# Side loads pinned in the queue, and a first pass of 18 groups in place of 19

## The chip, the cores and the metric

The kernel runs on one core of one Trainium2 chip. The metric is the device time of an execution in microseconds (us). The core's engines are TensorE (PE), VectorE (DVE), ScalarE (ACT), GpSimd (POOL) and SyncE (SP); here SP issues every transfer, so that SP's queue is the one order in which loads and stores start.

## The reference

Banded attention over q, k, v makes x (3072 x 512). A layer of 8 experts with dense routing follows; `P` is a softmax of `x @ w_gate` that is balanced by 8 rounds of row and column scaling.

```python
x = np.ascontiguousarray(attn_out.transpose(0, 2, 1, 3)).reshape(B * S, H * D)
...
    for e in range(E):
        h = np.maximum(x @ w1[e], 0.0)
        ye = h @ w2[e]
        out += P[:, e:e + 1] * ye
```

w1 is 8 x 512 x 1024, w2 is 8 x 1024 x 512, all of it float32.

## The kernel before

Every float32 operand is split into a high and a low part, and a product is three matmuls (high x low, low x high, high x high). Rows are handled in three blocks of 1024. The hidden dimension is cut into groups of 256; one group (two hidden tiles of one expert) was done during the attention already, so that 31 groups are left, numbered 0 to 30 (expert 0 has 3, each other expert 4).

Within a group both layers can use Strassen's scheme of seven products. Layer 1 always does: 7 products of 6 matmuls of 128x512, in the order x, y, x, z, w, z, w by the name of the PSUM bank. For layer 2 there are two forms. The **first pass** (block 2, `for g in range(SPLIT)`) uses the plain form: 8 row tiles of 6 matmuls (`y_ps`). The **later passes**, listed in `order`, are block 0 and block 1 with groups 0 to 30 each, and then the **return** of block 2 with groups `SPLIT` to 30; they use seven products of 6 matmuls in layer 2 (`m_ps`). TensorE alternates: a product of layer 1 of group g, then a piece of layer 2 of group g-1.

The later passes take the weights already summed, split and stored to DRAM (`w1s[g]`, `w2s[g]`). Who makes them:

- For groups below `SPLIT`, `make(g)` in the first pass, one group ahead: loads `w1f` and `w2f` (lines 740, 741), casts on ACT (L745), sums (L763) and low parts (L746) on POOL, and stores from `w1ops`, `w2ops`, `s2ops` (lines 790, 795, 796). It is needed by the first pass itself.
- For groups from `SPLIT` on, **side halves**: one half is the w1 or the w2 part of a group. `side_half` loads 512 KB into `raw` (L1454 for w2, L1461 for w1), a piece of `acc`. `quick` treats them beside the first pass: high parts (L1475, ACT), four sums on POOL (L763, `acc<-acc`), low parts (L1479, DVE), the high part of the sums (L1506, ACT, written over `raw`), their low part (L1508, DVE), and three stores: own parts (L1486, from `own`), high sums and low sums (both L1490, from `acc`). There is one `raw`, so that the next load waits until the store of the high sums has landed. `SPLIT - FIRST_SIDE - 1` halves are quick; the rest is `slow`, beside the pass of block 0, one half every two groups.

In the text the first load of `quick` stands in group 3 at step 6, each half is worked on in the group after its load, and its stores are at steps 4 and 5.

A scheduler orders each engine's instructions by its own estimate of when inputs are ready. `tc.keep_in_program_order(ins)` takes that freedom from one instruction in one direction: it is queued behind the instruction that stands just ahead of it in the text on the same engine. The matmuls are so pinned, and so are the first loads of the pass of block 0: `moe.in_order = True` holds when `load_first(w1s[0], ...)` and `load_x` are called, after the first pass. These are seven loads `w1r<-w1s` of 256 KB and seven loads `xr<-xs` of 1 MB (both L805).

`weights_of(n)` loads one expert's routing weights for a block (L1604, `acc<-p_dram`, 512 KB) into one of two pieces of `acc`; the piece for the first turn is the one that was `raw`.

Of the kernel before, what the change touches and what calls it, by code (L numbers as in the profile page):

```python
# [17 lines left out]
P = 128  # L18
# [21 lines left out]
FG = 2  # L40
# [1 line left out]
LATE = 2  # L42
TURNED = (0, 0, 1, 3, 4, 6, 7, 7)
FREE = 5
SPLIT = 19
FIRST_SIDE = 3
LOAD = 25
SIDE_END = 20
# [69 lines left out]
class Banded:  # L118
# [449 lines left out]
    def keep(self):  # L568

        if self.ended is None:  # L570
            return
        o_ps, g, x = self.ended
        self.ended = None
        of = o_ps.rearrange("p t c -> p (t c)")
        for xh, xl, src, dst, width, _ in x:
            self.nc.scalar.copy(out=xh[:, g, dst:dst + width], in_=of[:, src:src + width])
        for _, _, src, _, _, whole in x:
            if whole is not None:
                n, dst = whole[0], whole[1](g)
                self.nc.scalar.copy(out=dst, in_=of[:, src:src + n * P].rearrange("p (t q) -> p t q", q=P))  # L580
        for xh, xl, src, dst, width, _ in x:
            self.nc.vector.tensor_tensor(out=xl[:, g, dst:dst + width], in0=of[:, src:src + width],
                                         in1=xh[:, g, dst:dst + width], op=ALU.subtract)
# [11 lines left out]
class Dense:  # L595
# [19 lines left out]
    keep = flush  # L615
# [470 lines left out]
def pipeline(tc, attention, ident, moe, acc):  # L1086


    nc = tc.nc
    KT, KH, DM, NU, E = moe.KT, moe.KH, moe.DM, moe.NU, moe.E  # L1090
# [4 lines left out]
    groups = [(0, f) for f in range(NF0, FT, FG)] + [(e, f) for e in range(1, E) for f in range(0, FT, FG)]  # L1095
    NG = len(groups)
    PLAIN = NG - 1
    with ExitStack() as top:
# [227 lines left out]
        def make(g):  # L1326
            if g < SPLIT and g not in wts:
                s = staged if g == 0 else moe.stage_group(*groups[g], stage)
                wts[g] = moe.make_group(s, wpools[g % 2], spool[0], stage, w1s[g], w2s[g])
# [42 lines left out]
        def plain_ops():  # L1372
            hs = {}

            def ended(name, bank):
                hs[name] = hop.tile([P, 2, BU], F32R, name="hop")
                moe.relu_split(bank, hs[name])
            return hs, ended
# [66 lines left out]

        scratch = []

        def side_half(g, second):

            e, f = groups[g]  # L1450
            raw, sums, pair = (t.rearrange("p t d -> p (t d)") if n < 2 else t for n, t in enumerate(scratch[-1]))
            if second:
                src = moe.w2[e, f * P:(f + FG) * P, :].rearrange("(f p) d -> p f d", p=P)
                nc.sync.dma_start(out=raw.rearrange("p (f d) -> p f d", d=DM), in_=src)  # L1454
                rows = raw.rearrange("p (f e d) -> p f e d", f=2, e=2)
                a11, a12, a21, a22 = rows[:, 0, 0], rows[:, 1, 0], rows[:, 0, 1], rows[:, 1, 1]
                own = [((pair[:, 0, i], pair[:, 1:3, i]), (a11, rows[:, 1])) for i in range(2)]
                s = sums.rearrange("p (n d) -> p n d", n=4)
            else:
                src = moe.w1[e, :, f * P:(f + FG) * P].rearrange("(c p) f -> p c f", p=P)  # L1460
                nc.sync.dma_start(out=raw.rearrange("p (c f) -> p c f", f=FG * P), in_=src)  # L1461
                rows = raw.rearrange("p (o c e f) -> p o c e f", o=2, c=KH, e=FG)
                a11, a12, a21, a22 = rows[:, 0, :, 0], rows[:, 1, :, 0], rows[:, 0, :, 1], rows[:, 1, :, 1]
                wide = pair.rearrange("p o s (c f) -> p o s c f", f=P)
                own = [((wide[:, 0:2, i], wide[:, 2, i]), (rows[:, :, :, 0], a22)) for i in range(2)]
                s = sums.rearrange("p (n c f) -> p n c f", n=4, f=P)
            plain, more = second and g >= PLAIN, None
            if plain:
                more = sums[:, 0:2 * HD].bitcast(F32R).rearrange("p (s d) -> p s d", s=2)
                own = [((*t, more[:, i]), (*x, a21)) for i, (t, x) in enumerate(own)]  # L1470
            return raw, sums, pair, s, own, (a11, a12, a21, a22), plain, more

        def own_his(own):
            for t, x in zip(*own[0]):
                nc.scalar.copy(out=t, in_=x)  # L1475

        def own_lows(own, engine, keep=lambda ins: ins):
            for hi, lo, x in zip(own[0][0], own[1][0], own[1][1]):
                keep(engine.tensor_tensor(out=lo, in0=x, in1=hi, op=ALU.subtract))  # L1479

        def store_own(g, second, pair, more):
            if more is not None:
                nc.sync.dma_start(out=w2p[g - PLAIN][:, 0:3].bitcast(F32), in_=pair.bitcast(F32))
                nc.sync.dma_start(out=w2p[g - PLAIN][:, 3].bitcast(F32), in_=more.bitcast(F32))
            else:
                nc.sync.dma_start(out=(w2s if second else w1s)[g][:, 4:7].bitcast(F32), in_=pair.bitcast(F32))  # L1486

        def store_sums(g, second, part, t):
            dst = (w2s if second else w1s)[g][:, 0:4, part]
            nc.sync.dma_start(out=dst.bitcast(F32), in_=t.rearrange("p (n d) -> p n d", n=4))  # L1490

        def quick(halves):

            for g, second in halves:
                while (yield) != 6:
                    pass
                raw, sums, pair, s, own, parts, plain, more = side_half(g, second)
                while (yield) != 0:
                    pass
                own_his(own)  # L1500
                moe.left_sums(s, *parts, 0, 2)
                yield
                own_lows(own, nc.vector)
                moe.left_sums(s, *parts, 2, 4)
                yield
                nc.scalar.copy(out=raw.bitcast(F32R), in_=sums)  # L1506
                yield
                nc.vector.tensor_tensor(out=sums.bitcast(F32R), in0=sums, in1=raw, op=ALU.subtract)  # L1508
                while (yield) != 4:
                    pass  # L1510
                store_sums(g, second, 0, raw)
                store_own(g, second, pair, more)
                yield
                store_sums(g, second, 1, sums)
            scratch.append(None)
            while True:
                yield
# [37 lines left out]
        def beside(steps):  # L1555
            next(steps)
            return steps.send

        halves_late = [(g, second) for g in range(SPLIT, NG) for second in range(2)]
        quick_ones = SPLIT - FIRST_SIDE - 1  # L1560

# [6 lines left out]
        next(sinkhorn)  # L1568
        next(prev)
        side = beside(quick(halves_late[:quick_ones]))  # L1570
        for g in range(SPLIT):
            hs, ended = plain_ops() if g else lead
# [5 lines left out]
            def each(n):  # L1578
# [3 lines left out]
                if g > FIRST_SIDE or (g == FIRST_SIDE and n == 6):  # L1582
                    side(n)
                    if g > 3 and kept:
# [4 lines left out]
            prev = second_plain(b, g, w2, hs, lambda k: yps.tile([P, DM], F32, name="y_ps", tag="y"),  # L1589
                                g == SPLIT - 1, False, store=part_tile)  # L1590
        for _ in sinkhorn:
            pass
        for _ in turned:
            pass
        order = [(n, 0) for n in range(NB - 1)] + [(NB - 1, SPLIT)]
        cells = [(q, g) for q, (_, first) in enumerate(order) for g in range(first, NG)]
# [3 lines left out]
        def weights_of(n):  # L1600
            if n < len(turns) and turns[n] not in pbc:
                q, e = turns[n]
                t = acc[:, BT + 2 * (n % 2):BT + 2 * (n % 2) + 2]
                nc.sync.dma_start(out=t, in_=p_dram[order[q][0], :, e].rearrange("i j p -> i (j p)").partition_broadcast(P))  # L1604
                pbc[q, e] = t
# [34 lines left out]
        for q, (b, first) in enumerate(order):  # L1640
            x_ops, x_next = x_next, {}
            ms = {}
            for g in range(first, NG):
                e = groups[g][0]
                if g > first and groups[g - 1][0] == e:
                    weights_of(turns.index((q, e)) + 1)
                w = first_w.pop(g)
                if g < PLAIN:
# [89 lines left out]
def kernel(  # L1738
# [33 lines left out]
    with tc.If(rv > 0) as cmp:  # L1772
        pipeline(tc, band, ident, moe, acc)
    with cmp.Else():
        pipeline(tc, Dense(tc, q, k, v, ng, nl), ident, moe, acc)
# [32 lines left out]
```

## Time and profile before

| | |
|---|---|
| median of 3 runs | 2089.2 us (2088.31 to 2090.33) |
| the profiled execution, its own time | 2087.19 us |
| its span, from the first to the last instruction | 2085.2 us |
| PE busy | 2069.4 us, 99% of the span |
| POOL, DVE, ACT busy | 1609.1, 1541.7, 764.3 us |
| mean transfer rate | 248 GB/s |

The span is the profile's time axis; 2.0 us of the execution's own time lie outside it. The attention ends near 250 us, the first pass runs from there to 644.37 us, where the first matmul of block 0's pass starts. In a line of the timeline the numbers are start and duration in us, then engine, line, operation, tile written and tiles read; `[t <-X]` is idle time of the engine just before, and what ended it.

### The profile page before, as it was taken

The numbers are of one execution on the slowest core, as the hardware profiler recorded it, in microseconds if no ns is written. First come the engines' busy times: TensorE is split into PE (matmuls) and PEld (weight loads), VectorE is DVE, ScalarE is ACT, GpSimd is POOL, SyncE is SP. The second block draws the span as 40 slices with busy tenths as digits, with TensorE's granted clock in tenths as the row PEclk, the third lists the DMA queues.
The fourth block names the chain that finished last, engine by engine and source line by source line (L and its number), as shares of the span: only waits on it lengthen the run. The fifth ranks groups of instructions, "written<-read, shape, count | busy, mean of one in ns | idle before, by whom it ended". The sixth has DMA issues, their size and how long they took to land.

```text
span 2085.2 us, 31822 instructions
## 1 busy us (share of the span) xinstructions
PE 2069.4 (99%) x10401; PEld 1714.4 (82%) x10402; DVE 1541.7 (74%) x2291; ACT 764.3 (37%) x1604; POOL 1609.1 (77%) x1430
## 2 busy tenths in 40 slices
PE   9999999999999999999999999999999999999998
PEld 6888877888888888888888888888888888888887
DVE  7777688777775777777777775777777777767777
ACT  7898735444432322322322224222222222232221
POOL 5687698999973898998777776777777777767776
PEclk9999999999999999999999999999999999999999
DMA  6897798999989888888877788777777777797772
GB/s 145 203 234 213 235 376 310 346 340 353 335 317 368 282 251 265 266 255 276 267 204 194 204 304 282 202 203 200 199 203 204 194 204 204 219 365 204 193 194 91
DMA packets 351517, 516.15 MB, mean 248 GB/s; under 512 B 117297, under 2 KB 187121, under 8 KB 342385
## 3 DMA queue, kind: packets, MB, share of 16 engines
q1 hardware_dynamic: 351344, 514.02, 78.8%
q8 instruction: 87, 1.43, 0.3%
q14 instruction: 86, 0.70, 0.1%
HBM read 365.19 MB, written 148.73 MB: 246 GB/s over the span
## 4 chain that ended last, share of the span: by engine, by line
PE 96%; DVE 2%; POOL 1%; ACT 1%; DMA 0%; issue 0%; SPq 0%; ACTq 0%; POOLq 0%; DVEq 0%
PE m_ps L112 32%; PE y_ps L112 12%; PE bank_z L112 12%; PE bank_w L112 12%; PE bank_x L112 12%; PE bank_y L112 6%; PE o_ps L112 2%; PE s_ps L112 2%; PE t_ps L115 2%; PE h_ps L112 1%; PE tp L115 1%; PE r_ps L115 1%; PE c_ps L115 1%; DMA w1f<-in_moe_w_dram 0%; PE g_ps L112 0%
## 5 line engine op out<-in xcount | busy, mean ns | idle before, releaser
L112 PE MATMUL m_ps<-hop,w2r 128*128 128x512 f32 x2982 | 756.7, 389 | 0.0
L1709 DVE TENSOR_TENSOR m<-m_ps,m 128x1024 f32<-128x1024 f32 x476 | 580.4, 1220 | 228.8 <-PE m_ps L112 224.4
L112 PEld LDWEIGHTS m_ps<-hop,w2r 128*128 128x128 f32 x2982 | 559.8, 188 | 116.3
L1039 POOL TENSOR_TENSOR hop<-h,hop 128x512 fp32r<-128x512 f32 x213 | 276.8, 1299 | 294.8 <-ACT hop L1045 294.8
L1039 POOL TENSOR_TENSOR hop<-hsum,hop 128x512 fp32r<-128x512 f32 x284 | 362.0, 1298 | 2.9 <-ACT hop L1045 2.5
L1045 ACT CAST hop<-hsum 128x512 fp32r<-128x512 f32 x284 | 175.9, 622 | 467.7 <-POOL hsum L1039 464.3
L1045 ACT CAST hop<-h 128x512 fp32r<-128x512 f32 x213 | 132.4, 621 | 442.1 <-DVE h L1061 429.7
L112 PE MATMUL y_ps<-w2ops,hop 128*128 128x512 f32 x912 | 230.2, 391 | 2.3 <-DVE hop L882 2.3
L112 PE MATMUL bank_w<-xr,w1r 128*128 128x512 f32 x888 | 225.8, 390 | 0.0
L112 PE MATMUL bank_z<-xr,w1r 128*128 128x512 f32 x888 | 225.7, 389 | 0.0
L112 PE MATMUL bank_x<-xr,w1r 128*128 128x512 f32 x888 | 225.5, 389 | 0.0
L1039 POOL TENSOR_TENSOR hsum<-h,h 128x512 f32<-128x512 f32 x142 | 181.2, 1298 | 44.9 <-DVE h L1061 44.8
L112 PEld LDWEIGHTS y_ps<-w2ops,hop 128*128 128x128 f32 x912 | 171.7, 188 | 38.7 <-DVE hop L882 2.6
L112 PEld LDWEIGHTS bank_x<-xr,w1r 128*128 128x128 f32 x888 | 166.5, 188 | 34.5
L112 PEld LDWEIGHTS bank_w<-xr,w1r 128*128 128x128 f32 x888 | 166.4, 188 | 34.4
L112 PEld LDWEIGHTS bank_z<-xr,w1r 128*128 128x128 f32 x888 | 166.4, 188 | 34.4
L1039 POOL TENSOR_TENSOR hsum<-h,hsum 128x512 f32<-128x512 f32 x142 | 184.6, 1300 | 0.0
L1398 DVE SCALAR_TENSOR_TENSOR acc<-y_ps,pm,acc 128x512 f32<-128x512 f32 x152 | 113.2, 746 | 59.7 <-PE y_ps L112 59.1
L112 PE MATMUL bank_y<-xr,w1r 128*128 128x512 f32 x444 | 112.7, 389 | 0.0
L408 ACT ACTIVATE p_sb<-p_sb,mx 128x256 f32<-128x256 f32 (+1 forms) x192 | 93.6, 497 | 17.9 <-DVE mx L390 17.1
L112 PEld LDWEIGHTS bank_y<-xr,w1r 128*128 128x128 f32 x444 | 83.3, 188 | 17.3
L917 DVE TENSOR_TENSOR t<-bank_y,t 128x512 f32<-128x512 f32 x93 | 64.2, 690 | 38.2 <-PE bank_y L112 37.8
(224 smaller groups left out, 2977.9 us busy)
## 6 DMA issues: line engine op xcount, KB each, us to landing
w1r<-w1s SPq DMA_DIRECT2D x518, 256.0 KB, 3.0
w2r<-w2s SPq DMA_DIRECT2D x497, 256.0 KB, 3.0
w1s<-w1ops SPq DMA_DIRECT2D x19, 1792.0 KB, 7.2
w2s<-s2ops SPq DMA_DIRECT2D x19, 1024.0 KB, 7.7
w2s<-w2ops SPq DMA_DIRECT2D x19, 768.0 KB, 8.1
acc<-in_moe_w_dram SPq DMA_DIRECT2D x24, 512.0 KB, 5.7
w1s<-acc SPq DMA_DIRECT2D x24, 512.0 KB, 6.3
xr<-xs_t SPq DMA_DIRECT2D x12, 1024.0 KB, 11.2
```

Of the source, the lines that this page charges most:

```text
L112: return self.tc.keep_in_program_order(self.engine.matmul(*args, **kw))
L115: return self.tc.keep_in_program_order(self.engine.transpose(*args, **kw))
L408: nc.scalar.activation(out=pv, in_=pv, func=AF.Exp, bias=mx[:, u:u + 1], scale=-1.0, accum_out=sm[:, i, j:j + 1])
L917: tt(out=t, in0=bank["y"], in1=t, op=ALU.add)
L1039: ins = self.nc.gpsimd.tensor_tensor(out=out, in0=x, in1=y, op=ALU.subtract)
L1045: self.rounded = self.nc.scalar.copy(out=t[:, 0], in_=self.full[name])
L1398: nc.vector.scalar_tensor_tensor(out=a, in0=y_ps, scalar=moe.pm[:, tt, e:e + 1], in1=a, op0=ALU.mult, op1=ALU.add)
L1709: evicted[:] = [nc.vector.tensor_tensor(out=ms[p], in0=bank, in1=ms[p], op=ALU.add)]
```

## The change

`SPLIT` goes from 19 to 18: the first pass does 18 groups, the return 13 in place of 12, and side halves are made for groups 18 to 30: 26 in place of 24, of which 14 (before: 15) are quick and 12 (before: 9) are slow. The loads of `quick` go through `keep_in_program_order`; those of `slow` don't. The condition of `weights_of` is widened so that a pass that begins with the last group of an expert (group 18 is that of expert 4) also fetches the next expert's weights.

```diff
-SPLIT = 19
+SPLIT = 18
...
-        def side_half(g, second):
+        def side_half(g, second, keep=lambda ins: ins):
...
-                nc.sync.dma_start(out=raw.rearrange("p (f d) -> p f d", d=DM), in_=src)
+                keep(nc.sync.dma_start(out=raw.rearrange("p (f d) -> p f d", d=DM), in_=src))
...
-                nc.sync.dma_start(out=raw.rearrange("p (c f) -> p c f", f=FG * P), in_=src)
+                keep(nc.sync.dma_start(out=raw.rearrange("p (c f) -> p c f", f=FG * P), in_=src))
...
-                raw, sums, pair, s, own, parts, plain, more = side_half(g, second)
+                raw, sums, pair, s, own, parts, plain, more = side_half(g, second, tc.keep_in_program_order)
...
-                if g > first and groups[g - 1][0] == e:
+                if g > first and groups[g - 1][0] == e or g + 1 < NG and groups[g + 1][0] != e:
```

The call with `tc.keep_in_program_order` is the one in `quick`. In the orders below, `w1s_193` is `w1s[0]` and `w2s_224` is `w2s[0]`, and so on upwards by one for each group.

On SP, at the opening of the first pass, around the loads for `make(1)`; this is a piece of the difference:

```order
 L795 DMA w2s_224<-w2ops 128x1536
 L741 DMA w2f<-in_moe_w_dram 128x2x512
-L1461 DMA acc<-in_moe_w_dram 128x4x256
 L1586 DMA xs_t_182<-xh 128x2048
 L1586 DMA xs_t_181<-xh 128x2048
```

The first side load stood there, ahead of where the text has it; it has left this place. On SP of the changed kernel it now stands behind the last store of group 4's weights, just ahead of group 6's first store:

```order
L795 DMA w2s_228<-w2ops 128x1536
L741 DMA w2f<-in_moe_w_dram 128x2x512
L796 DMA w2s_228<-s2ops 128x2048
L1461 DMA acc<-in_moe_w_dram 128x4x256
L790 DMA w1s_199<-w1ops 128x3584
L1486 DMA w1s_211<-own 128x1536
```

So the side halves begin some four groups later, while their number falls by one. On SP at the end of the first pass, before:

```order
L1486 DMA w1s_219<-own 128x1536
L796 DMA w2s_240<-s2ops 128x2048
L1490 DMA w1s_219<-acc 128x4x256 x2
L1604 DMA acc<-p_dram 128x2x512
L790 DMA w1s_211<-w1ops 128x3584
L1604 DMA acc<-p_dram 128x2x512
...
L796 DMA w2s_242<-s2ops 128x2048
L805 DMA w1r<-w1s_193 128x512 x7
L805 DMA xr<-xs_b_164 128x2048
```

The same place in the changed kernel, where group 17 is the last group of the first pass:

```order
L796 DMA w2s_241<-s2ops 128x2048
L1486 DMA w1s_217<-own 128x1536
L1490 DMA w1s_217<-acc 128x4x256 x2
L1454 DMA acc<-in_moe_w_dram 128x2x512
L1486 DMA w2s_248<-own 128x1536
L1490 DMA w2s_248<-acc 128x4x256 x2
L805 DMA w1r<-w1s_193 128x512 x4
L1604 DMA acc<-p_dram 128x2x512
L805 DMA w1r<-w1s_193 128x512 x3
L805 DMA xr<-xs_b_164 128x2048
L805 DMA xr<-xs_t_168 128x2048
```

Before, the last side half's stores stood ahead of the weights of group 18, far ahead of the loads of block 0's pass. Now the stores of the last two halves, and the load of the last one, stand between the last weights of the first pass and those loads. In the built program the second `w1r` load also waits for the last store from `own` (its buffer takes that tile's place), and L1604 for the last store of high sums. On ACT of the changed kernel, at the end of the first pass:

```order
L745 CAST s2ops<-wsum_7661 128x4x256
L1475 CAST own<-acc 128x2x256
L1475 CAST own<-acc 128x256
L874 ACTIVATE hop<-bank_x 128x512
L1506 CAST acc<-acc 128x1024
L874 ACTIVATE hop<-bank_y 128x512
L874 ACTIVATE hop<-bank_z 128x512
L874 ACTIVATE hop<-bank_w 128x512
L1475 CAST own<-acc 128x256
L1475 CAST own<-acc 128x2x256
L1506 CAST acc<-acc 128x1024
L915 COPY t<-bank_x 128x512
```

The four `L874` are those of group 17, and `L915` is the first of block 0's pass: the last half but one is worked on within group 17, the last one behind it. Before, ACT's L1475 and L1506 don't occur in the last group and a half. POOL of the changed kernel has the sums of these two halves behind group 17's last instruction of `make`:

```order
L746 TENSOR_TENSOR w2ops<-w2f,w2ops 128x2x256 x2
L746 TENSOR_TENSOR s2ops<-wsum_7661,s2ops 128x4x256
L763 TENSOR_TENSOR acc<-acc 128x256 x8
L1039 TENSOR_TENSOR hop<-h_8043,hop 128x512
```

Before, `s2ops` of the last group was the last of POOL's work in the first pass, with `L1039` next.

In the first group of block 0's pass SP's order has changed too: before, each of the first pass's last stores (L1366, `yp<-acc`) was followed by one `w1r` and one `w2r` load; now the first six `w2r` loads stand together behind the seventh of these stores.

## Rows read from the trace of the kernel before

**Rows 1.** The page: its head, and the chain that ended last, by engine

```profile
span 2085.2 us, 31822 instructions
...
PE 96%; DVE 2%; POOL 1%; ACT 1%; DMA 0%; issue 0%; SPq 0%; ACTq 0%; POOLq 0%; DVEq 0%
```

**Rows 2.** Stretches: 3 us of group 1, a first-pass group, a later one

```profile
core 0: us, PE busy (x) PEld busy (x) DVE busy (x) ACT busy (x) POOL busy (x), PEclk, DMA share, GB/s
270.00:273.00 3.00, 2.64 (x6) 1.82 (x6) 1.00 (x3) 0.00 (x0) 3.00 (x4) 0.50 1.00 421
...
623.97:644.37 20.40, 20.40 (x92) 16.89 (x90) 11.97 (x18) 4.97 (x8) 4.90 (x3) 1.00 0.79 300
683.81:702.85 19.04, 19.04 (x86) 15.77 (x84) 13.41 (x16) 6.37 (x11) 18.59 (x18) 1.00 0.80 239
```

**Rows 3.** Timeline of PE in group 1

```profile
270.36 2.50 PE L112 MATMUL y_ps<-w2ops,hop 128*128 128x512 f32 x5 [2.30 <-DVE hop L882]
...
274.03 1.43 PE L112 MATMUL bank_y<-xh,w1ops 128*128 128x512 f32 x5 [0.75 <-POOL w1ops L746]
```

**Rows 4.** Waits of PE: in all, times, longest, in us

```profile
PE c_ps L112 <- DVE csum L1007: 1.8, 1, 1.8
```

**Rows 5.** Waits of SP, 585 to 665 us

```profile
SPq L1604 <- DMA w1s<-acc: 5.3, 1, 5.3
```

**Rows 6.** Timeline of SP: first side load, group 4's last store, end of the pass

```profile
253.90 1.24 SPq L1461 DMA_DIRECT2D acc<-in_moe_w_dram  x1
...
349.04 0.34 SPq L796 DMA_DIRECT2D w2s<-s2ops  x1
...
604.75 0.36 SPq L1604 DMA_DIRECT2D acc<-p_dram  x1
...
630.21 4.51 SPq L805 DMA_DIRECT2D w1r<-w1s  x7
634.84 0.36 SPq L805 DMA_DIRECT2D xr<-xs_b  x1
```

**Rows 7.** Timeline of POOL in group 1

```profile
269.38 1.59 POOL L763 TENSOR_TENSOR acc<-acc 128x256 f32<-128x256 f32 x2
...
271.62 2.35 POOL L746 TENSOR_TENSOR w1ops<-wsum,w1ops 128x1024 fp32r<-128x1024 f32 x1
```

**Rows 8.** Timeline of PE into and out of block 0's first group

```profile
641.65 2.88 PE L112 MATMUL y_ps<-w2ops,hop 128*128 128x512 f32 x12
644.37 1.52 PE L112 MATMUL bank_x<-xr,w1r 128*128 128x512 f32 x6
...
666.13 1.52 PE L112 MATMUL m_ps<-hop,w2r 128*128 128x512 f32 x6
```

**Rows 9.** Timeline of POOL: sums of a side half, and the last `make`

```profile
591.17 3.26 POOL L763 TENSOR_TENSOR acc<-acc 128x256 f32<-128x256 f32 x4
...
627.37 2.40 POOL L746 TENSOR_TENSOR s2ops<-wsum,s2ops 128x1024 fp32r<-128x1024 f32 x1
```

**Rows 10.** Timeline of ACT: a side half's cast, the last group's last ACTIVATE

```profile
594.81 1.05 ACT L1506 CAST acc<-acc 128x1024 fp32r<-128x1024 f32 x1 [5.03 <-DVE own L1479]
...
642.64 0.60 ACT L874 ACTIVATE hop<-bank_w 128x512 fp32r<-128x512 f32 x1 [2.18 <-DVE bank_w L930]
```

**Rows 11.** Landing of the stores of L1490, 240 to 640 us

```profile
DMA to landing us min/median/max: 2.9/6.6/10.5
```

**Rows 12.** Landing of the store of L796 issued at 629.79 us (1 MB)

```profile
DMA to landing us min/median/max: 5.0/5.0/5.0
```

**Rows 13.** Landing of the side load issued at 583.88 us (512 KB)

```profile
DMA to landing us min/median/max: 3.5/3.5/3.5
```

**Rows 14.** Timeline of DVE at the end of the first pass

```profile
643.88 0.68 DVE L882 SCALAR_TENSOR_TENSOR hop<-bank_w,hop 128x512 fp32r<-128x512 f32 x1
...
663.61 0.75 DVE L1398 SCALAR_TENSOR_TENSOR acc<-y_ps,pm,acc 128x512 f32<-128x512 f32 x1
```

**Rows 15.** All L1479 of the first pass (min/median/max in ns)

```profile
L1479 DVE TENSOR_TENSOR own<-acc,own x30: 413/1067/5351, 266.9 to 593.8; 128x512 fp32r<-128x512 f32 x15, 128x256 fp32r<-128x256 f32 x15
```

**Rows 16.** Landing of the seven `xr` loads, 634 to 660 us

```profile
DMA to landing us min/median/max: 7.2/10.0/15.1
```

**Rows 17.** The page's transfers: tile, engine, count, KB, us to landing

```profile
w2r<-w2s SPq DMA_DIRECT2D x497, 256.0 KB, 3.0
```

## The prediction

> **What bounds the kernel.** The page's head and its chain come first: TensorE (PE) carries 96% of the chain in a span of 2085.2 us [rows 1], so time comes off only where PE computes less or waits less. Then the stretches: a group fills PE completely at the full granted clock, in the first pass with 90 matmuls of the change's kind in 20.40 us and in a later pass with 84 in 19.04 us [rows 2]. The two group rows have 92 and 86 matmul records for 90 and 84 weight loads; I count 90 and 84. Then PE's waits: there are few, so I looked up the places that the side halves touch. In group 1 `y_ps` waits 2.30 us for DVE and, a little later, `bank_y` 0.75 us for POOL [rows 3]; PE's clock stands at 0.50, the lower level (1.2 GHz), for the 3 us around it [rows 2]. In group 3, where the first half is worked on, one `c_ps` waits 1.8 us [rows 4]. Last comes SP around 600 to 645 us, since the change moves its queue: there the only wait for a side store is the 5.3 us of L1604 [rows 5]. It ends at 604.75; the seven `w1r` loads follow only at 630.21, behind the last group's stores [rows 6]. So the side halves had ended a whole group before the first pass did.
>
> **What the change does, part by part.**
>
> *One group moves from the first form to the second.* 20.40 − 19.04 = **−1.4 us** [rows 2]. What comes with it (a load fewer in the first pass, a return group more) lies beside PE, as in every group.
>
> *The opening.* The first side load goes from group 1 to behind group 4's last store, and half 1 with it out of the groups that wait. In group 1, POOL does two sums of a side half in 1.59 us ahead of the `w1ops` that `bank_y` waits for [rows 7]. Without them `w1ops` comes 1.6 us earlier, and PE's `bank_y` can't come sooner than that although its 2.30 us wait goes: **−1.6 us**. If all of it vanished, with the half-clock loss, it would be 2.3 + 0.75 + 1.5 = 4.6; that is the bound. The 1.5 is what 3 us at 0.50 lose [rows 2]. The `c_ps` wait goes with the half that made it: **−1.8 us** [rows 4]; bound 0, if something else is late there.
>
> *The loads are late, and stay late.* There is one `raw`, and each load waits for a store of the half before. In the changed order the halves run at one a group, from about 349 us on instead of 254 [rows 6], and there are 14 instead of 15. So they can't be done a group before the end; by the orders, the last two fall into the last group and behind it. I work that out in the time axis of before, where the last group ends at 644.37 [rows 8].
>
> Half 13 of 14 (the last but one): POOL's sums stand behind `s2ops` of the last group, which ends at 627.37 + 2.40 = 629.77 [rows 9]. A half has four sums (the eight in the order are those of both halves); they take 3.26 [rows 9], to 633.0. L1506 on ACT takes 1.05 [rows 10], to 634.1. The high store must land before the next load: 2.9, 6.6 or 10.5 us as minimum, median and maximum [rows 11]. I take 5.0, what a 1 MB store took at this very place [rows 12]: 639.1.
>
> Half 14: its load lands 3.5 later, at 642.6 [rows 13]. Sums 3.26: 645.9. Its own high casts on ACT stand behind `hop<-bank_w`, which ends at 643.24 [rows 10]. Its low parts on DVE stand behind L882, which ends at 644.56 [rows 14], and are two instructions, each 0.41, 1.07 or 5.35 us as minimum, median and maximum [rows 15]; two medians give 646.7. The store from `own` lands 5.0 later, at 651.7. Beside this L1506 ends at 646.9 and its high store lands at 651.9.
>
> The second `w1r` load waits for the own store, and L1604 for the high store. Six `w1r` loads at 4.51/7 = 0.64 each are 3.9 us of issuing, L1604 0.4 more [rows 6]: the first `xr` load goes out at 651.7 + 3.9 + 0.4 = 656.0. `xr` lands 7.2 us later at best [rows 16]: 663.2. In the order of PE `bank_x<-xr` follows the last `y_ps` at once, and there is nothing else for PE to do. So PE stands still for 663.2 − 644.4 = **+18.8 us**. What is queued behind on SP are all loads of block 0's first groups.
>
> Bounds. With the shortest rows (stores 2.9, low parts 0.41 each) the load lands 2.1 sooner, which the low parts don't feel, since L882 holds them until 644.56. They end 1.3 sooner and their store lands 2.1 sooner: 18.8 − 3.4 = 15.4. With the median 6.6 for both stores [rows 11], the median 10.0 for `xr` [rows 16] and the longest low part (5.35 for one of the two) it is 18.8 + 1.6 + 1.6 + 2.8 + 4.3 = 29.
>
> One rule weighs on the low parts. The row shows the same instruction between 0.41 and 5.35 us [rows 15], without a reason beside it. The Trainium skill, "SBUF — State Buffer", section "SBUF: two separate sides", says that DVE and GpSimd share a port pair as an exclusive lock, and that an operation on DVE with two SBUF inputs waits out a GpSimd operation that reads SBUF. By that rule the low parts could start only after POOL's sums, at 645.9 and not 644.6, and the sum would be 1.3 us more. Another page, "DMA: Bandwidth & Descriptors", section "Anatomy of one DMA — SWDGE (gpsimd) path", gives 2.0 us plus bytes over 436e3 for a transfer, an estimate of 4.4 us for 1 MB; the row has 7.2 for `xr`, so by the page the sum would be 2.8 less. I stay with the rows.
>
> *After the wait.* After 2.3 us of idling the clock was 0.50 for about 3 us [rows 2, 3]; an idle of 19 us should bring that back: **+1.5** (1.2 to 1.7). In the first group of block 0's pass the `w2r` loads now stand together behind the seventh of the first pass's last `yp` stores, whose addition on DVE ends at 663.61 + 0.75 = 664.4 in the undisturbed axis [rows 14]. With 0.7 for store and issue and 3.0 for landing [rows 17] the first is there at 668.1, and `m_ps` wants it at 666.13 [rows 8]: **+2.0** (0 to 4).
>
> *At nothing:* three more slow halves beside block 0's pass. In a group of it, POOL is busy 18.59 of 19.04 us and PE still waits for nothing [rows 2]; what hides them is PE's own 19 us. Without that cover they would cost what POOL lacks, some 1 to 3 us in all.
>
> Sum against the profiled execution's own 2087.19 (its span plus 2.0): 2087.2 − 1.4 − 1.6 − 1.8 + 18.8 + 1.5 + 2.0 = 2104.7. The median of the runs lies 2.0 above that execution: 2106.7, said as **2107**.
>
> **The rivals.**
>
> *A, the pin only saves (faster).* The halves catch up, and only the savings stay: 2087.2 − 1.4 − 1.6 − 1.8 = 2082.4, plus 2.0: 2084. It decides at one point: the last side store must be out before `xr` is issued, and `xr` must land by 644.37, which leaves 644.37 − 634.84 − 7.2 = 2.3 us of slack to before [rows 6, 16]. For it: POOL idles through most of a first-pass group, 4.9 of 20.40 busy [rows 2]. Against it: in POOL's order two halves' sums stand behind the last `s2ops`, which ends at 629.77.
>
> *B, a short wait (about the same).* If the last half's load came two thirds of a group earlier than I think, the stall would be 5 us or so: 2084 + 5 + 1 = 2090.
>
> *C, more waits still (slower).* The late `w1r` and `xr` push the next groups' loads back too, or the twelve slow halves now reach groups in which POOL is full: 3 to 8 us on top, 2110 to 2115.
>
> *D, the pin changes nothing.* 13 of the 14 loads stand behind a store that the one `raw` forces in any case. It would leave −1.4 alone, 2088. The orders speak against it: the first load moves by four groups, and all after it hang on it.
>
> **How the numbers follow.** What a measurement of this kernel can tell from no change is about 0.2%, 4.2 us: 2085.0 to 2093.4. The late chain with my sizes has 0.75, C 0.16, B and D 0.05 together, A 0.04. Low end: shortest stall, opening at its bound, no `w2r` wait: 2087.2 − 1.4 − 4.6 − 1.8 + 15.4 + 1.2 + 2.0 = 2098, and 2 less, the spread of the runs shown: 2096. High end: stall 29 with the 2.0 and the 1.5 would be 2117; with part of C, 2119. Slower 0.92, same 0.04, faster 0.04.
>
> **What the profile after would show.** Right: PE idle before the first `bank_x<-xr` by 15 to 25 us, released by a DMA; SP waiting there for stores from `own` and `acc`; the clock at 0.50 behind it; no 2.30 us wait for DVE in group 1 and `c_ps` not in the list; an `m_ps<-w2r` wait of some 2 us. Wrong: if PE goes from `y_ps` to `bank_x<-xr` without idling, the chain of halves was faster than one a group and A or B holds; if PE idles there for less than 10 us, the landings or the sums are mis-sized; if the return or block 0's later groups last over 19.04 us, C adds. The forecast breaks most easily at the pace of the halves: it rests on each load waiting for a group, and two halves in one group would take 20 us off.

## The result, and the profile after

The changed kernel takes 2111.6 us (median of 4 runs, 2110.84 to 2114.84) against 2088.76 before (4 runs): a ratio of 1.0111, with a 95% interval of 1.0094 to 1.0129. It is slower by 22.8 us; 2107 was forecast, with a range of 2096 to 2119. The profiled execution took 2114.84, the longest of the four, and its span is 27.8 us longer than that of before.

PE's waits in the changed kernel (in all, times, longest, in us):

```profile
PE bank_x L112 <- DMA xr<-xs_b: 22.0, 1, 22.0
PE bank_z L112 <- DVE u L922: 4.2, 2, 3.5
PE bank_y L112 <- POOL w1ops L746: 2.7, 1, 2.7
PE m_ps L112 <- DMA w2r<-w2s: 2.6, 1, 2.6
```

The first line is the forecast stall. The 2.30 us for DVE in group 1 and the `c_ps` line have gone [rows 3, 4]. The fourth line is new; the second and third have grown, the third from 0.75 us [rows 3] and the second from this one before:

```profile
PE bank_z L112 <- DVE u L922: 0.7, 1, 0.7
```

PE's timeline where block 0's pass begins, and where its second product needs `w2r`:

```profile
646.89 2.92 PE L112 MATMUL bank_x<-xr,w1r 128*128 128x512 f32 x6 [21.97 <-DMA xr<-xs_b]
...
673.11 2.06 PE L112 MATMUL m_ps<-hop,w2r 128*128 128x512 f32 x6 [2.64 <-DMA w2r<-w2s]
```

Both rows are longer than the 1.52 us of such six matmuls before [rows 8]: behind each wait there are 3 us in which the granted clock is 0.50, the lower level (1.2 GHz), at once behind the first wait and 1 us later behind the second. The two stretches (columns as in [rows 2]):

```profile
646.89:649.89 3.00, 3.00 (x7) 2.42 (x8) 0.00 (x0) 0.04 (x1) 0.00 (x0) 0.50 1.00 423
...
674.20:677.20 3.00, 3.00 (x9) 2.33 (x8) 0.00 (x0) 1.40 (x2) 2.23 (x2) 0.50 1.03 397
```

What kept `xr` away stands in SP's timeline:

```profile
620.99 0.37 SPq L1454 DMA_DIRECT2D acc<-in_moe_w_dram  x1
627.47 0.33 SPq L1486 DMA_DIRECT2D w2s<-own  x1
629.13 1.62 SPq L1490 DMA_DIRECT2D w2s<-acc  x2
630.80 3.03 SPq L805 DMA_DIRECT2D w1r<-w1s  x4
633.87 0.43 SPq L1604 DMA_DIRECT2D acc<-p_dram  x1
634.35 3.44 SPq L805 DMA_DIRECT2D w1r<-w1s  x3
637.88 0.73 SPq L805 DMA_DIRECT2D xr<-xs_b  x1
```

The last side half is loaded at 620.99; PE has nothing left to do from 646.89 − 21.97 = 624.92 on; and the loads of block 0's pass go out only behind that half's stores.

The lengths of the groups on PE (from one first `bank_x` to the next) account for the 27.8 us. "Held DVE" is time that PE loses to single operations of DVE that take several us in place of 1 or less; they are looked at below.

| where | before | after | difference |
|---|---|---|---|
| start of group 0 | 249.73 | 250.38 | +0.7 |
| group 1 | 26.31 | 24.19 | −2.1 |
| groups 2 and 3 | 44.44 | 42.24 | −2.2 |
| held DVE: group 16 before; groups 11, 12 and 14 after, each over 20.40 | 1.0 | 5.2 | +4.2 |
| last group of the first pass, over 20.40 | 0.0 | 22.4 | +22.4 |
| first group of block 0's pass, over 20.40 | 0.0 | 1.7 | +1.7 |
| second group of block 0's pass, over 19.04 | 0.0 | 4.6 | +4.6 |
| one group moved | 20.40 | 19.04 | −1.4 |

### The profile page after: what moved, and what is told of

It is laid out like the page before. It is cut to its first block, busy times and chain, and to the rows that moved or that the text cites. A ratio compares the mean times of both kernels' runs of the same rounds, so it can differ in the third digit from the quotient of the medians.

```text
span 2113.0 us, 31861 instructions
## 1 busy us (share of the span) xinstructions
PE 2069.8 (98%) x10396; PEld 1715.0 (81%) x10396; DVE 1543.4 (73%) x2287; ACT 764.1 (36%) x1607; POOL 1620.3 (77%) x1444
## 4 chain that ended last, share of the span: by engine, by line
PE 89%; DMA 3%; POOL 3%; DVE 2%; issue 1%; ACT 1%; SPq 0%; POOLq 0%; DVEq 0%; ACTq 0%
PE m_ps L112 32%; PE bank_z L112 11%; PE bank_x L112 11%; PE bank_w L112 11%; PE y_ps L112 9%; PE bank_y L112 6%; PE o_ps L112 2%; PE s_ps L112 2%; PE t_ps L115 2%; PE h_ps L112 1%; DMA acc<-in_moe_w_dram 1%; PE tp L115 1%; POOL wsum L763 1%; POOL w1ops L746 1%; POOL acc L763 1%
## 5 line engine op out<-in xcount | busy, mean ns | idle before, releaser
L112 PE MATMUL m_ps<-hop,w2r 128*128 128x512 f32 x3024 | 767.9, 389 | 2.6 <-DMA w2r<-w2s 2.6
L1709 DVE TENSOR_TENSOR m<-m_ps,m 128x1024 f32<-128x1024 f32 x483 | 589.2, 1220 | 232.3 <-PE m_ps L112 228.5
L112 PEld LDWEIGHTS m_ps<-hop,w2r 128*128 128x128 f32 x3024 | 567.9, 188 | 120.9 <-POOL hop L1039 3.0
L1039 POOL TENSOR_TENSOR hop<-h,hop 128x512 fp32r<-128x512 f32 x216 | 280.1, 1297 | 286.6 <-ACT hop L1045 286.6
L1039 POOL TENSOR_TENSOR hop<-hsum,hop 128x512 fp32r<-128x512 f32 x288 | 366.5, 1293 | 5.9 <-ACT hop L1045 5.8
L112 PE MATMUL bank_x<-xr,w1r 128*128 128x512 f32 x900 | 230.0, 391 | 22.0 <-DMA xr<-xs_b 22.0
L112 PE MATMUL y_ps<-w2ops,hop 128*128 128x512 f32 x864 | 217.2, 390 | 0.0
L1039 POOL TENSOR_TENSOR hsum<-h,h 128x512 f32<-128x512 f32 x144 | 183.7, 1297 | 43.6 <-DVE h L1061 43.3
L112 PEld LDWEIGHTS bank_x<-xr,w1r 128*128 128x128 f32 x900 | 169.5, 189 | 57.5 <-DMA xr<-xs_b 22.4
L112 PEld LDWEIGHTS y_ps<-w2ops,hop 128*128 128x128 f32 x864 | 162.4, 188 | 34.3 <-DVE hop L882 0.2
L1039 POOL TENSOR_TENSOR hsum<-h,hsum 128x512 f32<-128x512 f32 x144 | 186.6, 1296 | 0.0
L1398 DVE SCALAR_TENSOR_TENSOR acc<-y_ps,pm,acc 128x512 f32<-128x512 f32 x144 | 107.3, 746 | 67.0 <-PE y_ps L112 65.4
```

What stands on the lines that cost most here:

```text
L112: return self.tc.keep_in_program_order(self.engine.matmul(*args, **kw))
L1039: ins = self.nc.gpsimd.tensor_tensor(out=out, in0=x, in1=y, op=ALU.subtract)
L1398: nc.vector.scalar_tensor_tensor(out=a, in0=y_ps, scalar=moe.pm[:, tt, e:e + 1], in1=a, op0=ALU.mult, op1=ALU.add)
L1709: evicted[:] = [nc.vector.tensor_tensor(out=ms[p], in0=bank, in1=ms[p], op=ALU.add)]
```

## The experiments

Each was compared with the kernel before, run beside it on the same chip in five rounds, where nothing else is said. "Changed" is the changed kernel.

| kernel | median us | ratio, 95% interval |
|---|---|---|
| 18 groups, no pin | 2091.8 | 1.0018 (1.0009 to 1.0027) |
| the pin alone, 19 groups | 2115.2 | 1.0132 (1.0117 to 1.0146) |
| changed, first load a group earlier | 2093.6 | 1.0033 (1.0023 to 1.0043) |
| changed, first load two groups earlier | 2103.2 | 1.0074 (1.0060 to 1.0089) |
| 18 groups, no pin, pools exchanged | 2087.2 | 0.9998 (0.9988 to 1.0008) |
| 19 groups, pin, 12 quick halves | 2087.3 | 1.0003 (0.9992 to 1.0015) |
| 18 groups, pin, a group earlier, 13 quick halves, pools exchanged | 2087.3 | 0.9998 (0.9987 to 1.0009) |
| changed, L1604 behind `xr` | 2106.7 | 1.0089 (1.0072 to 1.0106) |
| 18 groups, pin, a group earlier, 13 quick halves, pools exchanged, low parts on POOL | 2091.2 | 1.0024 (1.0011 to 1.0037) |
| 19 groups, pin, 12 quick halves, low parts on POOL | 2108.8 | 1.0099 (1.0085 to 1.0114) |
| 18 groups, pin, 13 quick halves, pools exchanged, sums on DVE | 2088.4 | 1.0007 (0.9998 to 1.0016) |

### One part of the change at a time

Without the pin:

```diff
-                raw, sums, pair, s, own, parts, plain, more = side_half(g, second, tc.keep_in_program_order)
+                raw, sums, pair, s, own, parts, plain, more = side_half(g, second)
```

> The changed kernel without the pin: 18 groups in the first pass, 14 quick and 12 slow halves, loads of quick halves free again. Theory (the late first load makes the whole loss): the first side load returns to group 1, the last side store goes out a group before the first pass ends, PE does not stand still before block 0's first matmul, and only the moved group's 1.4 us remains: 2087.4 us (2085.5 to 2090), PE's 2.3 us wait for DVE in group 1 and the c_ps wait in group 3 as before. Rival (the split itself costs: three more slow halves, a return of 13 groups, the widened condition): 2095 us or more, with waits of PE in block 0's pass or in the return.

Measured 2091.8. The stall before `bank_x` is gone and the waits of the opening are back, but the kernel is slower than before by some 4 us, where 1.4 less was expected. Its waits of PE:

```profile
PE m_ps L112 <- DMA w2r<-w2s: 2.6, 1, 2.6
PE y_ps L112 <- DVE hop L882: 2.3, 1, 2.3
PE c_ps L112 <- DVE csum L1007: 1.8, 1, 1.8
```

So the `w2r` wait belongs to the 18 groups and not to the pin. The pin alone (`SPLIT = 19`):

> The pin alone: 19 groups in the first pass as before, 15 quick halves, loads pinned. Theory (the late first load makes the whole loss): a stall of PE of 18 to 26 us before block 0's first matmul, the opening cheaper by some 4 us: 2113 us (2107 to 2119). Rival (the split makes the loss): no stall there, 2085 to 2089 us.

Measured 2115.2; there is no `w2r` wait, and the stall is this:

```profile
PE bank_x L112 <- DMA xr<-xs_b: 24.1, 1, 24.1
```

With this many quick halves the pin makes the stall. In the built programs, pinning the first load alone gives the same order on all five engines as pinning all of them, and pinning all but the first the same as pinning none; these two were not run, so that no measurement shows it. By these orders the other loads hang on the first, as forecast.

### When the chain of halves ends

The first load is moved ahead in the text, by one group and by two; the number of quick halves stays 14:

```diff
-FIRST_SIDE = 3
+FIRST_SIDE = 2
...
-        quick_ones = SPLIT - FIRST_SIDE - 1
+        quick_ones = SPLIT - FIRST_SIDE - 2
```

> The changed kernel with the first quick load one group earlier in the text (group 2, step 6, still pinned); again 14 quick and 12 slow halves. Theory (a matter of when the chain of halves ends): the last side stores then lie within the last group and ahead of its last two stores of weights; of the 22 us stall 0 to 3 us are left, no half clock behind it: 2085 us (2082 to 2090). Rival (the loads of block 0's first operands are slow at this place whatever stands ahead of them, so that a group more of time does not help): a stall of 10 us or more is left, 2097 us or more.

Measured 2093.6. Of the 22 us, 3.5 are left, a little more than the 0 to 3 expected, so that the theory holds for most of the stall; but the time is outside what was expected: the `w2r` wait of 3.0 and the half clock behind both waits are there as well. What keeps the 3.5 was not tested; both L1604 stand ahead of the `w1r` loads there, and the first `w1r` lands 10.0 us after its issue. One group further (`FIRST_SIDE = 1`, minus 3):

> The same with the first quick load two groups earlier (group 1, step 6, pinned), 14 quick and 12 slow halves. Theory: no stall before block 0's first matmul; the first half is worked on near group 2 and 3 again, so that one of the waits of the opening (c_ps, 1.8 us) may come back: 2085 us (2082 to 2089), at most 2 us from the kernel that starts at group 2. Rival (an early side load is what costs at the opening): 2 to 5 us more than the kernel that starts at group 2.

Measured 2103.2, against the expectation; its profiled execution took 2100.25. Its profile has three things beside the `w2r` wait: `c_ps` waits 1.1 again; a DVE operation is held in the middle of the pass (below) and costs 6.5 in one group; and a wait of 3.8 before `bank_x` stays. The last probably comes from the last `w2f` load, which took 12 us to land behind the L1604 loads, so that POOL waited 8.8 us for it and the last stores of weights went out late; no run moves that load.

### The w2r wait

In the built program the first `w2r` tiles lie where `w2ops` of the odd groups lies (no run here shows the addresses). Even and odd groups alternate between two pools. With 19 groups the last one is even; with 18 it is group 17, whose `w2ops` are read until the eighth `y_ps` in block 0's first group. In the trace of the changed kernel the first `w2r` loads go out as that `y_ps` (the second half of the first row) ends:

```profile
666.23 2.88 PE L112 MATMUL y_ps<-w2ops,hop 128*128 128x512 f32 x12
...
668.94 2.83 SPq L805 DMA_DIRECT2D w2r<-w2s  x6
```

The two pools were exchanged, so that `mpool`, which is first written a group later, lies there:

```diff
-        mpool = top.enter_context(tc.tile_pool(name="mpool", bufs=7, side="right", reuse_waits="tile"))
         w2r = top.enter_context(tc.tile_pool(name="w2r", bufs=12, side="right", reuse_waits="tile"))
+        mpool = top.enter_context(tc.tile_pool(name="mpool", bufs=7, side="right", reuse_waits="tile"))
```

> The kernel with 18 groups and without the pin, and with the places of two pools in SBUF exchanged: the one of the w2r tiles is opened ahead of mpool, so that its first tiles no longer lie where w2ops of the odd groups lay (the last group of the first pass is now an odd one, and its w2ops are read until the eighth y_ps of block 0's first group). Theory (that place makes the w2r loads wait): the m_ps wait of 2.6 us and the half clock behind it, 4.5 us together, are gone; 2087.3 us against 2091.8 without the exchange (2085.5 to 2089.5). Rival (the w2r loads are late because of the transfers around them): the wait stays, 2091 to 2092 us.

Measured 2087.2, 4.6 less than without the exchange (4.2 by the two ratios). The first `w2r` load goes out at 629.02, where without the exchange it did at 644.97, and PE goes through that place without a wait:

```profile
629.02 0.42 SPq L805 DMA_DIRECT2D w2r<-w2s  x1
...
644.88 1.52 PE L112 MATMUL bank_x<-xr,w1r 128*128 128x512 f32 x6
646.24 1.52 PE L112 MATMUL m_ps<-hop,w2r 128*128 128x512 f32 x6
```

### The length of the stall

In the text, `weights_of(0)` goes behind the `xr` loads; its load now goes through `moe.fetch`, which pins it there while `moe.in_order` holds:

```diff
-        weights_of(0)
         moe.pe = attention.pe
...
         for load in (moe.load_first(w1s[0], w1r, first_w[0]), load_x(order[0][0], x_next)):
             for _ in load:
                 pass
+        weights_of(0)
         moe.in_order = False
```

> The changed kernel with the first load of routing weights (L1604) called behind the xr loads in place of ahead of the w1r loads, and pinned there. Theory (in the profile after, the L1604 that stands among the w1r loads holds the transfers behind it up for some 3.6 us, which I had put at 0.4): the stall of 22.0 us shrinks to 17.5 to 19.5, 2108 us (2106.5 to 2110). Rival (it is the stores of the last half alone): the stall stays at 21 to 23 us, 2111 to 2113 us.

Measured 2106.7, and the stall as expected:

```profile
PE bank_x L112 <- DMA xr<-xs_b: 18.3, 1, 18.3
```

### Can the pin pay?

> 19 groups as before, loads pinned, but 12 quick and 12 slow halves in place of 15 and 9. Theory (the pin itself is cheap, only the end of the chain of halves costs): the last side stores go out a group and a half before the end, both L1604 a group before it, no stall before block 0's first matmul; the opening saves the 1.9 us of group 1 and the 2.0 us of group 3: 2083.5 us (2081.5 to 2087). Rival (pinned loads cost by themselves, wherever the chain ends; or twelve slow halves do): 2088 us or more.

> 18 groups, pinned, the first quick load one group earlier, 13 quick and 13 slow halves (the loads of acc that stood in group 25 of a pass stand in group 27), and w2r ahead of mpool. Theory: as with 19 groups and 12 quick halves, and 1.4 us less for the moved group: 2082 us (2080 to 2086); against the kernel with the first load one group earlier alone (2093.6) the stall of 3.5 us before bank_x, the m_ps wait of 3.0 and the half clock behind each are gone. Rival (13 slow halves reach groups in which they cost): 2088 us or more, with waits of PE after group 20 of block 0's pass.

```diff
-        quick_ones = SPLIT - FIRST_SIDE - 1
+        quick_ones = SPLIT - FIRST_SIDE - 4
```

(The diff is the first's, with `SPLIT = 19`; the second has `FIRST_SIDE = 2`, minus 3, `LOAD = 27` and the exchange of pools.) Both medians are 2087.3: no change that can be told. The stall is under 1 us in their profiles and the opening is cheaper, so that the profiled executions took 2084.4 and 2081.4, each the shortest of its runs; but the runs reach from 2084.4 to 2096.0 and from 2081.4 to 2094.5. The kernel before is not still either: beside them it reached from 2085.9 to 2093.8. The last one once more:

> A second look at the kernel with 18 groups, first load a group earlier, 13 quick halves and the exchanged pools, whose profiled execution took 2081.4 us and whose median is 2087.3. Theory (a held L1479 in some executions): if this execution takes over 2085 us, its profile shows in one or two groups of the first pass an L1479 of over 5 us with POOL busy all along, and PE waiting for DVE there. Rival: it takes over 2085 us with the first pass as before and the time elsewhere.

It took 2083.1, so that it doesn't tell the two apart: the longest L1479 in its profile is 2.3 us, and 2.4 in the other:

```profile
L1479 DVE TENSOR_TENSOR own<-acc,own x26: 473/1086/2382, 322.2 to 569.8; 128x512 fp32r<-128x512 f32 x13, 128x256 fp32r<-128x256 f32 x13
```

The 1.7 us between these two executions of one kernel lie in group 1, which took 24.06 and 25.75 us, and not in a held operation.

The suspect was a held DVE operation. In the profile of the changed kernel the longest is in group 14. The timeline of DVE, POOL and PE there, in order of time:

```profile
549.60 0.78 POOL L763 TENSOR_TENSOR wsum<-wsum,w1f 128x256 f32<-128x256 f32 x1
549.70 6.04 DVE L1479 TENSOR_TENSOR own<-acc,own 128x256 fp32r<-128x256 f32 x1 [1.50 <-ACT own L1475]
550.30 1.47 POOL L763 TENSOR_TENSOR acc<-acc 128x256 f32<-128x256 f32 x2
551.69 2.41 POOL L746 TENSOR_TENSOR s2ops<-wsum,s2ops 128x1024 fp32r<-128x1024 f32 x1
554.01 0.76 POOL L763 TENSOR_TENSOR wsum<-w1f,wsum 128x256 f32<-128x256 f32 x1
554.69 1.63 POOL L763 TENSOR_TENSOR acc<-acc 128x256 f32<-128x256 f32 x2
...
556.40 0.50 PE L112 MATMUL bank_z<-xl,w1ops 128*128 128x512 f32 x1 [3.55 <-DVE u L922]
```

An operation that takes 0.4 us at its shortest takes 6.0 beside a POOL that works on and on, and PE waits for what is queued behind it on DVE. When it ends can be read from the single records: most of POOL's follow each other with an overlap, but behind 555.46 there are 0.08 us in which POOL does nothing, and L1479 ends at 555.74. That is so for all eleven operations of DVE over 4 us between 240 and 700 us in the fourteen traces: POOL's first gap since they began, often of 0.08 us, comes 0.1 to 1.1 us before their end. The 5.35 us of [rows 15] is one of them (its gap is at 593.29, its end at 593.84). Two edits were tried against it. Low parts on POOL:

```diff
-                own_lows(own, nc.vector)
+                own_lows(own, nc.gpsimd)
```

> The kernel with 18 groups, first load a group earlier, 13 quick halves and the exchanged pools, and with the low parts of the quick halves (L1479) on POOL in place of DVE. Theory (what is left of the spread, 2081 to 2094 us, comes from DVE being held in L1479 while POOL works without a gap, so that PE's banks wait for DVE): the runs lie closer together, 2081 to 2087, and their median near the best profiled execution, 2083 us (2081 to 2086). Rival (the spread has another cause): the spread and the median of 2087.3 stay, or POOL's longer queue makes the weights late and it is slower.

> The kernel with 19 groups, pinned loads and 12 quick halves, with the low parts of the quick halves on POOL in place of DVE. Theory: as above, median 2084.5 us (2083 to 2087) and a spread under 6 us where it was 11.5 (2084.4 to 2096.0). Rival: 2087 us with the spread as it was.

Both expectations fell: 2091.2 and 2108.8, with the spread no smaller in the first (2089.9 to 2100.5; the second reaches from 2106.4 to 2111.1). POOL was busy 19.2 of 20.4 us a group and is now busy 20.2, so that it has hardly a gap left, and L1508 is held in L1479's place. The timeline of the second kernel, of DVE and of POOL:

```profile
413.94 1.43 POOL L763 TENSOR_TENSOR wsum<-w2f 128x256 f32<-128x256 f32 x2
415.10 12.45 DVE L1508 TENSOR_TENSOR acc<-acc 128x1024 fp32r<-128x1024 f32 x1 [0.90 <-ACT acc L1506]
...
424.13 2.33 POOL L746 TENSOR_TENSOR s2ops<-wsum,s2ops 128x1024 fp32r<-128x1024 f32 x1
433.96 1.44 POOL L763 TENSOR_TENSOR wsum<-w1f 128x256 f32<-128x256 f32 x2 [7.50 <-DMA w1f<-in_moe_w_dram]
```

L1508, 1.2 us at its shortest, begins while POOL works and ends at 427.55, 1.1 us after POOL first stops (426.46). In that kernel PE then waits 12.4 us for DVE in all, and 6.0 for `xr`. The other way round, the sums of the quick halves on DVE:

```diff
-                moe.left_sums(s, *parts, 0, 2)
+                moe.left_sums(s, *parts, 0, 2, engine=nc.vector)
```

(and the same for sums 2 to 4.)

> The kernel with 18 groups, first load a group earlier, 13 quick halves and the exchanged pools, with the four sums of a quick half on DVE in place of POOL; the low parts on DVE again. Theory (DVE is held where POOL works without a gap; POOL is busy 19.2 of 20.4 us a group there and would be busy 16): gaps in POOL's work come sooner, no operation of DVE is held over 4 us, the runs lie closer together, 2081 to 2087, median 2083.5 us (2081 to 2086). Rival (more operations of DVE that read two tiles of SBUF are more that can be held): 2088 us or more, with PE waiting for DVE in the first pass.

Measured 2088.4. The spread is less than half (2086.2 to 2091.6, 5.4 for 13.1), but so is that of the kernel before on this other chip (3.4 us, for 7.9 beside the 13.1). With POOL busy 16 us and less a group no operation is held over 4 us; the two profiles without this edit have none either. All L1479, and the sums on DVE (minimum, median and maximum in ns):

```profile
L1479 DVE TENSOR_TENSOR own<-acc,own x26: 409/678/2612, 324.3 to 574.3; 128x512 fp32r<-128x512 f32 x13, 128x256 fp32r<-128x256 f32 x13
...
L763 DVE TENSOR_TENSOR acc<-acc x52: 405/414/2716, 322.0 to 573.3; 128x256 f32<-128x256 f32 x52
```

But the median isn't lower: DVE is late for PE by small amounts in groups 3, 5 and 8 (`c_ps` 1.5 us, `bank_z` 2.0 us in two waits). No version beats the kernel before by what can be measured.

## Why the prediction was right, and where its terms were off

**The mechanism is the one forecast.** The pinned first load comes late (the first L1479 runs at 355.1 us and not at 266.9 [rows 15]), all halves follow, and the last of them holds SP's queue. The last group starts 19.84 us earlier than in the axis used in the working (604.13 for 623.97). In that axis shifted by 19.84, the forecast chain and the measured one are:

| step | forecast | measured |
|---|---|---|
| high store of half 13 landed | 619.3 | 621.0 |
| load of half 14 landed | 622.8 | 624.5 |
| low parts of half 14 done | 626.9 | 627.4 |
| its own store landed | 631.9 | 631.8 |
| its high store landed | 632.1 | 633.1 |
| first `xr` load issued | 636.2 | 637.9 |
| it landed | 643.4 | 646.9 |

**How near, and how much of it is luck.** The sum gave 2104.7 us for the profiled execution, and this took 2114.84, some 10 more: +3.6 at the stall with the rest of its group, +2.6 at the `w2r` loads, +4.2 by held operations of DVE, +0.7 ahead of group 0, +0.2 by the clock, −0.9 at the opening. The median missed by 4.6 only, since it lies 3.2 below that execution, where the forecast put it 2.0 above. It also lies in the 2110 to 2115 of rival C, whose mechanism did not occur (below).

**The stall, +18.8, measured 22.0.** The step that was too small is the last: six `w1r` and L1604 were counted by their issue, 3.9 and 0.4 us, and `xr` by a landing of 7.2 [rows 16]. The issue took 6.1 (637.9 − 631.8), 2.45 of it for the last `w1r` alone, and the landing 9.0. Landings of the four `w1r` loads ahead of L1604, of L1604, of the three behind it, and of the first `xr` load (minimum, median, maximum):

```profile
DMA to landing us min/median/max: 4.0/4.5/5.4
...
DMA to landing us min/median/max: 8.5/8.5/8.5
...
DMA to landing us min/median/max: 8.7/8.8/9.0
...
DMA to landing us min/median/max: 9.0/9.0/9.0
```

L1604 moves 512 KB, twice a `w1r` tile, and everything behind it lands some 4 us later. Taken out of the way, the stall is 18.3. The Trainium skill, "DMA: Bandwidth & Descriptors", section "Anatomy of one DMA — SWDGE (gpsimd) path", gives 4.4 us, an estimate, for one transfer of 1 MB that GpSimd issues; here SP issues it, and with a queue ahead of it the trace has 9.0. In the bounds, the high end counted 1.6 us for a later landing of half 13's store, most of which the low parts would not have felt, since L882 held them longer by the same working; 29 is too high by about that.

**The rule on the low parts.** The working took the rule that the Trainium skill, "SBUF — State Buffer", section "SBUF: two separate sides", states for one instruction as holding the low parts until all four of POOL's sums end. In the changed kernel these sums run from 624.62 to 628.03, and the two low parts end at 627.44, for 626.9 by the rows and 628.2 by the working's reading: they began behind L882 at 625.66 and took 1.78 us together, and were not held to the end. In groups 11, 12 and 14 operations of DVE are held through three to five of POOL's, and the price of 1.3 us at one place was far too low for what this did elsewhere.

**The opening, −1.6 and −1.8, measured −2.1 and −2.2** (group 1; groups 2 and 3). In group 1 `bank_y` now waits 2.7 us for `w1ops`, so that POOL is the limit there, as the working said. The −2.1 is that of one pair of executions: group 1 takes 24.0 to 25.8 us in the eleven profiles with the pin, and 26.3 to 28.0 in the three without.

**The clock, +1.5, measured 1.7.** It stood at 0.50 for 3 us after the idle time.

**The w2r loads, +2.0, measured 4.6.** The wait is 2.6; the half clock that follows it costs another 1.9 and was not counted. The place was read rightly from the order, the reason wasn't given; the exchange of pools shows it: which of the two alternating pools the last group uses, and so the parity of the number of groups.

**Not forecast: held operations of DVE,** +4.2 in the profiled execution against the one of before. Rival C named more waits and put them in block 0's pass, at the slow halves; they came in the first pass, at the quick ones. Three more slow halves cost nothing: every group of block 0's pass from the third to the last but one takes 19.04.

**The other rivals.** A (only savings) would need the chain to end a group or more earlier; with 12 and 13 quick halves the profiled executions come near the 2084 it gave, the medians don't. What was said for it, a POOL busy for 4.9 of 20.40 us, is a row of the last group, in which POOL makes no weights for a next one; in a group in the middle of the first pass it has hardly a gap:

```profile
541.38:561.78 20.40, 20.40 (x91) 16.89 (x90) 15.22 (x21) 8.71 (x14) 19.09 (x19) 1.00 0.96 356
```

B (a short wait) fits the kernel with the first load a group earlier, 3.5 us of stall, and not this one. D (the pin changes nothing) is refuted by the pin alone.

**What stays open.** That held operations of DVE make the spread of the pinned versions, 12 to 13 us between runs, is not shown. For it speak the two profiles without one (2081.4 and 2083.1). The smaller spread with the sums on DVE says little, since the kernel before spread less on that chip too, and group 1 alone differs by 1.7 us between two executions of one kernel. No long execution of those versions has a profile.

## What to carry to other kernels

A queue that issues in order turns the start of a side chain into its end: if the chain runs at one piece per stage, a later first load moves the last store by as much, and what stands behind that store in the queue is the price, so work out the last piece against the next stage's first load before pinning the first one. Count a stage boundary by landings and not by issues, with every slow transfer ahead in the queue. And where buffers alternate, changing the number of rounds by one changes which buffer is still in use when the next stage's tiles take its place.

## What was not expected of the hardware

An operation of DVE with two SBUF inputs can be held through a whole series of GpSimd operations: 6.0 us through five rows of POOL, and 12.45 us through eight, where the longest single POOL operation took 2.4. In the first of the two kernels with low parts on POOL a copy with one input (L1020) was held too, for 6.5 us. The Trainium skill, "SBUF — State Buffer", section "SBUF: two separate sides", has the lock for a whole instruction; here the waiting DVE operation did not get it between two instructions of POOL that followed each other without a gap. In each of the eleven long holds it came through behind the first gap in POOL's work, and 0.08 us were enough. The hold is not certain: at the end of the first pass a low part got through beside four sums. Moving work to GpSimd to relieve DVE made this worse (holds of up to 10.6 and 12.45 us, for 6.1 at most in the twelve other profiles). That moving work away makes it better is not shown: 2.7 us at most with the sums on DVE, 2.4 without that edit.
